# Sliding-window branch: two heads per evacuation, query copies on GpSimd, and the late weight loads on another queue

## The chip, the cores and the metric

One core of one Trainium2 chip runs the whole program. The metric is the device time of one execution in microseconds; a lower time is better. The kernel before takes 2685.36 us (median of three runs, 2685.33 to 2692.31).

## The reference

Two attention branches read the same 2048 x 640 input and a gate mixes them:

```python
g = sigmoid((x * gate_w).sum(-1))
a = A(x)        # 32 heads of width 20, query i sees keys i-255..i, output projection 640 x 640
b = B(x, mem0)  # 64 segments of 32 tokens, one after the other, 32 heads of width 192
out = g * a + (1 - g) * b
```

In branch B each segment is joined with 8 memory tokens, goes through the projections Wq, Wk, Wv, attention and Wo, and its first 8 output rows are the memory of the next segment. So the 64 segments form a chain. All tensors are bfloat16.

## The kernel before, in words

The program has four stages, one after the other on TensorE.

**The sliding branch** (`branch_A`) walks over 16 query blocks of 128 rows. A block sees up to `nk` = 3 key blocks of 128 keys (1 in the first block, 2 in the second). For each of the 32 heads there are three steps. `st_scores` makes the 128 x 384 scores in one PSUM bank (three products and two more that add the masks), VectorE takes the row maximum (`a_nmx`), and ScalarE writes the exponentials (`a_ex`). `st_transpose` turns the three 128 x 128 pieces on TensorE into a PSUM tile `pt_ps`, and one instruction copies that tile to SBUF (`a_pt`): ScalarE for two heads of three, VectorE for the third. `st_pv` multiplies with the values into `o_ps`. The loop over `i` issues scores of head `i`, the transpose of head `i-3` and the value product of head `i-5`. The scores have five PSUM buffers, `pt_ps` has two (pool `ps_t`), `o_ps` has one.

A query block needs its projections first. `prep_units` gives them as seven pieces, and the pieces for block `qb+1` are put between the heads of block `qb`. The query piece (`mk_qk` with `isq`) writes `QT_blk` on ScalarE and then four copies `QTm` per 16 heads (20 partitions x 512 elements each, the other partitions stay zero), eight copies in a block. `QTm` exists twice, so those of block `qb+1` are written while block `qb` computes. At the end of a block the result is transposed (`aT_ps`), copied (`aT`), multiplied with `wo` (`out_ps`), scaled by the gate (`ga`) and stored.

GpSimd has little to do in a block: it clears and fills `xs`, writes the column of ones of `V_blk`, and in the first blocks it issues DMAs: the first 30 weight tiles of branch B that stay in SBUF (`early`), and the copies of the streamed tiles into a packed DRAM tensor (`w_packed`).

**The tail products** (`tail_projections`) project the last 8 rows of every segment ahead of time, because they do not depend on the memory. First come the q and k products: four groups `g`, four column tiles `t`, six PSUM tiles of 20 products each (`t_psum`), copied alternately by ScalarE and VectorE to a staging tile `t_qk` (two buffers), which SyncE stores to DRAM as `xbqk`. Then come the v products (`t_psv`, `t_vt`, three buffers, stored as `xbv`). PSUM has eight tiles for both. One weight tile of each q and k group is streamed through `w_ring`.

Ahead of that stage the program loads the next weight tiles (`late`), and behind it the last two (`last`). Both are issued on SyncE's queue. A q, k or v tile is one DMA, an o tile is four.

**The memory branch** (`branch_B`) is a chain of 64 segments in an order written out by a planner of its own; it streams 21 weight tiles per segment from `w_packed` on SyncE's queue. **The mix** (`mix_out`) ends the program.

Outside of branch B the framework sets the order of the instructions on each engine: it lists them by the order in which they are written and by when its own plan has them ready, so the order in a queue differs from the text of the program. Each queue is then executed strictly in that order, and an instruction that waits holds up all behind it.

The lines that the change touches are 130 to 132 (query copies), 198 to 208 (transposes and their copies), 229 to 235 (the loop), 859 (the split of the weight tiles) and 880 to 887 (their loads).

Of the kernel before, what the change touches and what calls it, by code (L numbers as in the profile page):

```python
# [9 lines left out]
BF = mybir.dt.bfloat16  # L10
# [7 lines left out]
def branch_A(tc, x, wqkv, wo, gate_w, spread_x, ga_dram, omg_dram, W=256, HA=32, extra_units=None):  # L18
    nc = tc.nc
    S, D = x.shape  # L20
    P = 128
    KT = D // P
    DH = D // HA
    NB = S // P
    NG = HA // 4
    NKB = W // P + 1
# [3 lines left out]
    with ExitStack() as ctx:  # L30
# [50 lines left out]
        qms = {}  # L81

        def prep_units(qb):
# [31 lines left out]
            def mk_qk(isq, g0):  # L115
                def u():
                    xT = stt['xT']
                    Wp = WqP if isq else WkP
                    ng = min(4, NG - g0)
                    pst = ps_s.tile([P, 512], FP32, name="qk_ps", tag="s")  # L120
                    for gg in range(ng):
                        g = g0 + gg
                        for kt in range(KT):
                            nc.tensor.matmul(pst[:, gg * P:(gg + 1) * P],  # L124
                                             lhsT=Wp[:, kt, 4 * g:4 * g + 4, :].rearrange("p h d -> p (h d)"),
                                             rhs=xT[:, kt, :], start=(kt == 0), stop=(kt == KT - 1))
                    src = pst[:, 0:ng * P].rearrange("p (g q) -> p g q", q=P)
                    if isq:
                        nc.scalar.mul(stt['QT'][:, g0:g0 + ng, :], src, scale)
                        for r in range(4):  # L130
                            nc.vector.tensor_copy(qms[qb][r][32 * r:32 * r + DH, g0:g0 + ng, :],
                                                  stt['QT'][32 * r:32 * r + DH, g0:g0 + ng, :])
                    else:
                        nc.vector.tensor_copy(stt['KTb'][:, g0:g0 + ng, :], src)  # L134
                        if g0 + ng >= NG:
                            kring[qb] = stt['KTb']
                return u
# [27 lines left out]
        for qb in range(NB):  # L165
# [30 lines left out]
                hs[h] = dict(ex=ex)  # L196

            def st_transpose(h):
                ex = hs[h]['ex']
                pt_ps = ps_t.tile([P, NKB, P], BF, name="pt_ps", tag="t")  # L200
                for ci in range(nk):
                    nc.tensor.transpose(pt_ps[:, ci, :], ex[:, ci * P:(ci + 1) * P], ident[:])  # L202
                pt = hp.tile([P, NKB, P], BF, name="a_pt")
                if h % 3 != 2:
                    nc.scalar.copy(pt[:, 0:nk, :], pt_ps[:, 0:nk, :])  # L205
                else:
                    nc.vector.tensor_copy(pt[:, 0:nk, :], pt_ps[:, 0:nk, :])
                hs[h]['pt'] = pt

            def st_pv(h):  # L210
                pt = hs[h]['pt']
# [14 lines left out]
            nu = len(nxt)  # L226
            every = max(1, (HA - 4) // max(1, nu))
            ui = 0
            for i in range(HA + 5):
                if i < HA:  # L230
                    st_scores(i)
                if 0 <= i - 3 < HA:
                    st_transpose(i - 3)
                if 0 <= i - 5 < HA:
                    st_pv(i - 5)
                if ui < nu and i >= 2 and (i - 2) % every == 0:
                    nxt[ui](); ui += 1
# [20 lines left out]
P = 128  # L258
# [566 lines left out]
def kernel(  # L825
# [30 lines left out]
    xo_dram = dram.tile([nseg, P, KT * SEG], BF, name="xo_dram")  # L856
    streamed = [(k, g, c) for k in KINDS for g in range(4) for c in STREAMED[k][g]]
    weights = Weights(nc, dram, B_Wq, B_Wk, B_Wv, B_Wo, streamed)
    early, late, last = weights.resident[:30], weights.resident[30:-2], weights.resident[-2:]
    pre = ctx.enter_context(tc.tile_pool(name="b_pre", bufs=1))  # L860
    units = [lambda u=u: weights.load_resident(pre, u, nc.gpsimd) for u in early]
    units += [lambda u=u: weights.pack(u, nc.gpsimd) for u in streamed]
    with tc.tile_pool(name="b_xtail", bufs=1) as xtail:
        xTb = xtail.tile([P, KT, nseg * MEM], BF, name="xTb")
        with tc.tile_pool(name="b_xs", bufs=2) as xsp:

            def spread_x(qb, xT):
                n = P // SEG
                xv = xT[:].rearrange("p k (s a t) -> p s a k t", s=n, t=MEM)
                xs = xsp.tile([P, n, KT, SEG], BF, name="xs")  # L870
                nc.gpsimd.memset(xs[:], 0.0)
                for i in range(n):
                    nc.gpsimd.tensor_copy(xs[:, i, :, MEM:SEG], xT[:, :, i * SEG:(i + 1) * SEG - MEM])
                nc.sync.dma_start(xa_dram[qb * n:(qb + 1) * n].rearrange("s p c -> p s c"),
                                  xs[:].rearrange("p s k t -> p s (k t)"))
                nc.gpsimd.tensor_copy(xTb[:, :, qb * n * MEM:(qb + 1) * n * MEM].rearrange("p k (s t) -> p s k t", t=MEM), xv[:, :, 3])

            branch_A(tc, x, A_wqkv, A_wo, gate_w, spread_x, ga_dram[:], omg_dram[:], extra_units=units)
        post = ctx.enter_context(tc.tile_pool(name="b_post", bufs=1, side="right"))
        for u in late:  # L880
            weights.load_resident(post, u, nc.sync)
        tail_projections(tc, weights, xTb, xbqk, xbv)

    with ExitStack() as inner:
        end = inner.enter_context(tc.tile_pool(name="b_end", bufs=1))
        for u in last:
            weights.load_resident(end, u, nc.sync)
        branch_B(inner, tc, xa_dram, xbqk, xbv, mem0, weights, xo_dram)
    mix_out(tc, xo_dram, omg_dram[:], ga_dram[:], outf)

# [34 lines left out]
```

## Time and profile before

| | |
|---|---|
| median of three runs | 2685.36 us |
| the profiled execution | 2690.68 us, span 2689.0 us |
| sliding branch | 0 to 559.6 us |
| tail products | 559.6 to 771 us |
| memory branch and mix | 771 to 2689 us |
| busy share of the span | TensorE 85%, VectorE 45%, ScalarE 43%, GpSimd 18% |
| mean granted TensorE clock | 0.921 |

The stages are read from the timeline: the first tail product starts at 559.6 us, and the first streamed weight load of the memory branch is issued at about 771 us. The busy shares are averages over stages with different limits. From one full-size block of the sliding branch to the next everything in the trace returns after 34.1 to 34.4 us; the last such step takes 38.6 us.

### The profile page before, as it was taken

To read this page: it belongs to the slowest core of one execution; us is meant where nothing else is said; L and a number is where in the kernel's file an instruction comes from. 1 tells how busy PE (TensorE), PEld (TensorE's weight loads), DVE (VectorE), ACT (ScalarE), POOL (GpSimd) and SP (SyncE) were. 2 spreads that over 40 slices of the span, in tenths; PEclk is the share of its full clock that TensorE was granted. 3 is DMA by queue.
4 is the path that set the end of the run, shared out by engine and by line. 5 is a ranking of instruction groups with operands and counts; after the bars stand their busy time and mean duration, and the time that the engine had idled before them with its cause. 6 is when DMAs were issued, how large, how long until landed. Compare 5 with 4: busy or idle time off the path is not lost.

```text
span 2689.0 us, 114071 instructions
## 1 busy us (share of the span) xinstructions
PE 2289.0 (85%) x49893; PEld 1690.2 (63%) x49893; DVE 1212.2 (45%) x3738; ACT 1156.9 (43%) x2657; POOL 484.0 (18%) x1579
## 2 busy tenths in 40 slices
PE   6888888858978888888888888898888888888885
PEld 5777777657745665566566665666565656566663
DVE  6777777622233443443443443343344334334433
ACT  4777777722223333333333333343333333334333
POOL 6300000000011212222222222222222222122210
PEclk9888888888988988999999999899999999899987
DMA  7300000055568888888888888888888888888887
GB/s 275 103 17 17 17 17 14 10 169 159 146 207 258 269 268 264 287 283 279 279 273 292 281 272 273 276 283 285 275 272 274 271 272 276 259 277 280 281 263 232
DMA packets 303060, 591.78 MB, mean 220 GB/s; under 512 B 102552, under 2 KB 115616, under 8 KB 302560
## 3 DMA queue, kind: packets, MB, share of 16 engines
q1 hardware_dynamic: 282752, 537.49, 63.4%
q0 software_dynamic: 16848, 43.54, 5.0%
q8 instruction: 391, 6.41, 1.0%
q10 hardware_dynamic: 2960, 3.44, 0.4%
q14 instruction: 109, 0.89, 0.1%
HBM read 554.98 MB, written 36.97 MB: 220 GB/s over the span
## 4 chain that ended last, share of the span: by engine, by line
PE 51%; DMA 32%; ACT 9%; DVE 4%; issue 3%; SPq 1%; POOL 0%; ACTq 0%; DVEq 0%; POOLq 0%
DMA t_w<-w_packed 29%; PE ps_q L592 8%; PE ps_k L592 8%; PE ps_o L757 8%; PE ps_v L592 5%; ACT a_ex L195 4%; PE t_psum L433 3%; ACT a_pt L205 2%; PE ps_pv L733 2%; PE tr_k L607 2%; PE qk_ps L124 2%; PE pt_ps L202 2%; PE out_ps L250 2%; PE S_ps L661 2%; PE t_psv L450 1%
## 5 line engine op out<-in xcount | busy, mean ns | idle before, releaser
L592 PEld LDWEIGHTS <-t_hT 128*32 128x32 bf16 x15360 | 382.0, 99 | 316.2 <-issue 108.7
L757 PE MATMUL ps_o<-t_OT,t_w 128*128 128x40 bf16 x6400 | 270.5, 182 | 120.3 <-DMA t_w<-w_packed 110.4
L757 PE MATMUL ps_o<-t_OT,w_o 128*128 128x40 bf16 x8960 | 335.1, 182 | 41.7 <-ACT t_OT L738 41.7
L195 ACT ACTIVATE a_ex<-s_ps,a_nmx 128x384 bf16<-128x384 f32 (+2 forms) x512 | 288.9, 613 | 76.4 <-DVE a_nmx L193 76.0
L757 PEld LDWEIGHTS <-w_o 128*128 128x128 bf16 x8960 | 289.9, 98 | 49.1 <-issue 43.2
L757 PEld LDWEIGHTS <-t_w 128*128 128x128 bf16 x6400 | 210.7, 98 | 149.3 <-DMA t_w<-w_packed 146.2
L738 ACT CAST t_OT<-ps_pv 128x480 bf16<-128x480 f32 x256 | 142.9, 558 | 336.0 <-PE ps_pv L733 335.9
L193 DVE TENSOR_REDUCE a_nmx<-s_ps 128x1 f32<-128x384 f32 (+2 forms) x512 | 253.9, 525 | 29.8 <-PE s_ps L190 21.4
L597 ACT CAST t_tok<-ps_k 128x384 bf16<-128x384 f32 x256 | 122.5, 478 | 317.6 <-PE ps_k L592 317.6
L716 DVE TENSOR_TENSOR t_PTx<-PT_ps,mk_x 128x320 bf16<-128x320 f32 x256 | 125.2, 489 | 270.4 <-PE PT_ps L709 270.4
L592 PE MATMUL ps_q<-w_q,t_hT 128*32 128x384 bf16 x4096 | 229.7, 348 | 18.7 <-DVE t_hT L768 18.4
L592 PE MATMUL ps_v<-w_v,t_hT 128*32 128x384 bf16 x4352 | 231.7, 337 | 0.0
L639 POOL COPY t_K<-t_xqk 128x64 bf16<-128x64 bf16 x256 | 60.4, 236 | 950.5 <-PE S_ps L661 671.3
L592 PE MATMUL ps_k<-w_k,t_hT 128*32 128x384 bf16 x4096 | 228.0, 345 | 0.0
L187 PE MATMUL s_ps<-KT_blk,QTm 128*128 128x128 bf16 x1440 | 193.0, 227 | 2.5 <-DVE KT_blk L134 1.7
L202 PE MATMUL pt_ps<-a_ident,a_ex 128*128 128x128 bf16 x1440 | 161.4, 220 | 39.2 <-ACT a_pt L205 24.7
L630 DVE COPY t_K<-tr_k 128x256 bf16<-128x256 bf16 x256 | 74.0, 289 | 262.2 <-PE tr_k L607 260.9
L597 ACT CAST t_tok<-ps_q 128x384 bf16<-128x384 f32 x256 | 122.9, 480 | 145.0 <-PE ps_q L592 144.6
L205 ACT COPY a_pt<-pt_ps 128x384 bf16<-128x384 bf16 (+2 forms) x352 | 175.3, 508 | 18.2 <-PE pt_ps L202 13.9
L597 ACT CAST t_vtok<-ps_v 128x384 bf16<-128x384 f32 x256 | 122.4, 478 | 118.1 <-PE ps_v L592 117.4
L607 PEld LDWEIGHTS <-t_tok 128*128 128x128 bf16 x1536 | 88.1, 98 | 118.7 <-issue 55.4
L768 DVE CAST t_hT<-ps_o 128x40 bf16<-128x40 f32 x63 | 12.6, 200 | 320.9 <-PE ps_o L757 320.9
(136 smaller groups left out, 4601.3 us busy)
## 6 DMA issues: line engine op xcount, KB each, us to landing
t_w<-w_packed SPq DMA_DIRECT2D x704, 384.0 KB, 4.2
t_w<-w_packed SPq DMA_DIRECT2D x640, 320.0 KB, 4.2
xbqk<-t_qk SPq DMA_DIRECT2D x16, 768.0 KB, 4.3
t_xqk<-xbqk POOLq DMA_DIRECT2D x64, 192.0 KB, 4.7
w_v<-in_B_Wv_dram SPq DMA_DIRECT2D x17, 384.0 KB, 9.1
w_q<-in_B_Wq_dram POOLq DMA_DIRECT2D x16, 384.0 KB, 7.1
xbv<-t_vt SPq DMA_DIRECT2D x64, 96.0 KB, 1.8
t_xv<-xbv POOLq DMA_DIRECT2D x128, 48.0 KB, 4.5
```

The source lines that it names most:

```text
L187: nc.tensor.matmul(sp[:, ci * P:(ci + 1) * P], lhsT=qm[r][:, g, :], rhs=kring[c][:, g, :], start=True, stop=not need_mask)
L193: nc.vector.tensor_reduce(out=nmx[:], in_=sp[:, 0:nk * P], axis=AX.X, op=ALU.max, negate=True)
L195: nc.scalar.activation(out=ex[:, 0:nk * P], in_=sp[:, 0:nk * P], func=ACT.Exp, bias=nmx[:], scale=1.0)
L202: nc.tensor.transpose(pt_ps[:, ci, :], ex[:, ci * P:(ci + 1) * P], ident[:])
L205: nc.scalar.copy(pt[:, 0:nk, :], pt_ps[:, 0:nk, :])
L433: nc.tensor.matmul(pt[:, bb, :], lhsT=ws[ki][kt][:, c:c + P], rhs=xTb[:, kt, t * P:(t + 1) * P], start=(kt == 0), stop=(kt == KT - 1))
L592: nc.tensor.matmul(t[32 * j:32 * j + 32, 0:384], lhsT=tile_of(hT)[:, kt, :], rhs=w[:, j * 384:(j + 1) * 384], start=(kt == kts[0]), stop=( ...
L597: sc.op("ACT", act(384), lambda: nc.scalar.copy(tile_of(tok)[:], b["tile"][:, 0:384]), reads=[b], writes=[tok])
L607: nc.tensor.transpose(t[:, k, :], tok["tile"][:, k * P:(k + 1) * P], ident[:])
L716: nc.vector.tensor_tensor(out=tile_of(dst)[:], in0=PT["tile"][:, i, :, :].unsqueeze(2).to_broadcast([P, 2, 4, L]), in1=mk.unsqueeze(1).uns ...
L738: sc.op("ACT", act(480), lambda: nc.scalar.copy(tile_of(OT)[:].rearrange("p b j l -> p (b j l)"), o["tile"][:, 0:480]), reads=[o], writes= ...
L757: nc.tensor.matmul(t[:, dt * L:(dt + 1) * L], lhsT=w[:, r * D + dt * P:r * D + (dt + 1) * P], rhs=OT["tile"][:, b, i, :], start=(g == 0 an ...
```

## The change

Three things change.

1. Transposes and their copies go by pairs of heads. `st_transpose` does nothing for an even head; for an odd head it transposes both heads of the pair into one PSUM tile of twice the size and copies it with one instruction, ScalarE for every other pair and VectorE for the rest. The copied tile has four buffers of two heads in place of eight of one. `st_pv` runs for two heads in every second turn of the loop.
2. The eight query copies `QTm` of a block are issued on GpSimd in place of VectorE.
3. Four more weight tiles are loaded early (34 in place of 30), and the remaining `late` and `last` loads are issued on GpSimd's queue in place of SyncE's.

```diff
@@ mk_qk
                         for r in range(4):
-                            nc.vector.tensor_copy(qms[qb][r][32 * r:32 * r + DH, g0:g0 + ng, :],
+                            nc.gpsimd.tensor_copy(qms[qb][r][32 * r:32 * r + DH, g0:g0 + ng, :],
                                                   stt['QT'][32 * r:32 * r + DH, g0:g0 + ng, :])
@@ st_transpose
             def st_transpose(h):
-                ex = hs[h]['ex']
-                pt_ps = ps_t.tile([P, NKB, P], BF, name="pt_ps", tag="t")
-                for ci in range(nk):
-                    nc.tensor.transpose(pt_ps[:, ci, :], ex[:, ci * P:(ci + 1) * P], ident[:])
-                pt = hp.tile([P, NKB, P], BF, name="a_pt")
-                if h % 3 != 2:
-                    nc.scalar.copy(pt[:, 0:nk, :], pt_ps[:, 0:nk, :])
+                if h % 2 == 0:
+                    return
+                pt_ps = ps_t.tile([P, 2, NKB, P], BF, name="pt_ps", tag="t")
+                for a in range(2):
+                    ex = hs[h - 1 + a]['ex']
+                    for ci in range(nk):
+                        nc.tensor.transpose(pt_ps[:, a, ci, :], ex[:, ci * P:(ci + 1) * P], ident[:])
+                pt = hp.tile([P, 2, NKB, P], BF, name="a_pt", bufs=4)
+                if h % 4 == 1:
+                    nc.scalar.copy(pt[:, :, 0:nk, :], pt_ps[:, :, 0:nk, :])
                 else:
-                    nc.vector.tensor_copy(pt[:, 0:nk, :], pt_ps[:, 0:nk, :])
-                hs[h]['pt'] = pt
+                    nc.vector.tensor_copy(pt[:, :, 0:nk, :], pt_ps[:, :, 0:nk, :])
+                for a in range(2):
+                    hs[h - 1 + a]['pt'] = pt[:, a]
@@ the loop over heads
-            for i in range(HA + 5):
+            for i in range(HA + 6):
                 if i < HA:
                     st_scores(i)
                 if 0 <= i - 3 < HA:
                     st_transpose(i - 3)
-                if 0 <= i - 5 < HA:
+                if 0 <= i - 5 < HA and i % 2 == 0:
+                    st_pv(i - 6)
                     st_pv(i - 5)
@@ the kernel
-    early, late, last = weights.resident[:30], weights.resident[30:-2], weights.resident[-2:]
+    early, late, last = weights.resident[:34], weights.resident[34:-2], weights.resident[-2:]
@@
         for u in late:
-            weights.load_resident(post, u, nc.sync)
+            weights.load_resident(post, u, nc.gpsimd)
         tail_projections(tc, weights, xTb, xbqk, xbv)
@@
         for u in last:
-            weights.load_resident(end, u, nc.sync)
+            weights.load_resident(end, u, nc.gpsimd)
```

## The prediction

> **What bounds the kernel now.** I read the page first, then windows by stage, then the chain of waits inside one block of the sliding branch, the grouped lines by form, and the queues of SyncE and GpSimd around the tail products.
>
> ```profile
> PE 2289.0 (85%) x49893; PEld 1690.2 (63%) x49893; DVE 1212.2 (45%) x3738; ACT 1156.9 (43%) x2657; POOL 484.0 (18%) x1579
> ...
> 0.00:559.60 559.60, 474.82 (x7120) 398.82 (x7121) 397.88 (x1018) 413.31 (x961) 88.27 (x213) 0.90 0.18 58
> 559.60:771.00 211.40, 164.85 (x2261) 141.30 (x2261) 50.95 (x81) 43.19 (x80) 6.54 (x25) 0.89 0.58 166
> 771.00:2689.00 1918.00, 1649.35 (x40520) 1150.09 (x40511) 763.35 (x2639) 700.40 (x1616) 389.15 (x1341) 0.93 0.86 273
> ```
>
> Columns of a window: length, busy of PE, PE loads, DVE, ACT, POOL, clock, DMA share, GB/s. The change touches the first two rows, 771 us; the third (1918 us) has the same instructions before and after, and I put it at zero. In the first row ACT and DVE are busy 74% and 71%, far above their 43% and 45% of the page.
>
> One block of the sliding branch, from the chain of waits and the waits of two blocks:
>
> ```profile
> by line: ACT a_ex L195 19.3%; ACT a_pt L205 11.5%; PE qk_ps L124 11.1%; PE pt_ps L202 8.7%; PE out_ps L250 8.1%; PE s_ps L187 7.2%; DVE a_nmx L193 6.1%; issue 6.0%; PE s_ps L190 4.9%; DVE a_pt L207 2.8%; DVE QTm L131 2.5%; PE o_ps L217 2.3%
> ...
> 445.45 0.37 ACT a_pt L205
> ...
> 448.48 0.36 DVE a_pt L207
> ...
> 448.89 0.34 PE pt_ps L202 x3
> ...
> 449.31 0.49 ACT a_pt L205
> ...
> 455.49 0.11 PE s_ps L187
> ...
> ACT a_ex L195 <- DVE a_nmx L193: 9.7, 6, 4.1
> PE pt_ps L202 <- ACT a_pt L205: 3.3, 8, 0.7
> ```
>
> A block has 27 us in which heads run (scores from 421.4, one 34.1 us period before 455.49, to the last exponential at 448.48) and 7 us of ending (448.48 to 455.49: last copy, value product, `aT`, `out_ps`). In the 27 us ScalarE waits little: of its 9.7 us in two blocks for the row maximum, 4.1 per block is the block's first. It is the bound there, with VectorE close behind.
>
> ```profile
> L205 ACT COPY a_pt<-pt_ps 128x384 bf16<-128x384 bf16 x286 | 146.3, 521 | 15.4 <-PE pt_ps L202 11.8 <-remote 2.9 <-PE s_ps L190 0.2
> ...
> L207 DVE COPY a_pt<-pt_ps 128x384 bf16<-128x384 bf16 x130 | 45.7, 351 | 18.7 <-ACT a_ex L195 18.3
> ...
> L205 ACT COPY a_pt<-pt_ps 128x256 bf16<-128x256 bf16 x22 | 8.3, 394 | 1.3 <-PE pt_ps L202 1.2
> ...
> L207 DVE COPY a_pt<-pt_ps 128x256 bf16<-128x256 bf16 x10 | 2.9, 285 | 1.5 <-PE pt_ps L202 1.3
> ...
> 432.07 1.18 DVE L131 COPY QTm<-QT_blk 20x512 bf16<-20x512 bf16 x4
> ...
> 433.95 0.22 PE L187 MATMUL s_ps<-KT_blk,QTm 128*128 128x128 bf16 x1
> ...
> 434.48 0.22 PE L187 MATMUL s_ps<-KT_blk,QTm 128*128 128x128 bf16 x1
> ```
>
> The tail products, on SyncE's queue, TensorE, GpSimd's queue and the chain:
>
> ```profile
> 562.51 14.73 SPq L382 DMA_DIRECT2D w_v<-in_B_Wv_dram  x17
> 577.88 34.49 SPq L387 DMA_DIRECT2D w_o<-in_B_Wo_dram  x48
> 612.49 6.90 SPq L442 DMA_DIRECT2D xbqk<-t_qk  x3
> ...
> 617.69 0.58 PE L433 MATMUL t_psum<-xTb,w_q 128*128 128x128 bf16 x4 [35.47 <-ACT t_qk L438]
> ...
> 617.69 6.09 PE t_psum L433 x80
> ...
> 624.88 6.24 DMA w_ring<-w_packed
> ...
> 631.17 73.81 PE t_psum L433 x1316
> ...
> 761.82 1.12 SPq L387 DMA_DIRECT2D w_o<-in_B_Wo_dram  x2
> ...
> 770.54 4.32 SPq L560 DMA_DIRECT2D t_w<-w_packed  x5
> ...
> 771.05 5.18 DMA t_w<-w_packed
> ...
> 779.59 0.27 PE S_ps L654
> ...
> 769.84 0.57 POOL L546 DMA_DIRECT2D t_xqk<-xbqk  x1 [3.71 <-DMA xbv<-t_vt]
> ```
>
> The first three stores of `xbqk` stand behind 65 load issues and leave at 612.49, though the tiles were ready long before. Both `t_qk` buffers are full, the eight PSUM tiles fill, and TensorE stops for 35.47 us, from 582.2 to 617.7.
>
> **The change part by part.**
>
> *Copies by pairs.* ScalarE issues 21.3 copies a block at 0.37 us from start to start, 7.9 us. From 256 to 384 elements a copy grows by 127 ns, so 384 more cost 0.38 us: eight copies of 0.75 us, 6.0 us. ScalarE gains 1.9 us a block. VectorE goes from 10.7 copies of 0.26 (0.36 in the chain less the 0.1 us by which the next begins early), 2.8 us, to eight of 0.46 (66 ns per 128 elements, 0.20 us more each), 3.7 us: it loses 0.9 us. TensorE issues the same products. Each `pt_ps` buffer now holds two heads, so the wait of `pt_ps` for ScalarE's copy (3.3 us in two blocks) should shrink. In the ending, the last transposes no longer wait for VectorE's copy of the head two before (0.36 us), but there are six and their copy is longer (351 + 198 = 549 ns on VectorE against 490): I count nothing.
>
> *Query copies.* VectorE loses eight at 0.29 us, 2.35 us a block; with the 0.9 above it gains 1.4. On GpSimd:
>
> ```profile
> L876 POOL COPY xTb<-xT_blk 128x160 bf16<-128x160 bf16 x16 | 5.2, 325 | 0.0
> ...
> L66 POOL COPY WkP<-wqk_stage 128x640 bf16<-128x640 bf16 x5 | 4.1, 828 | 4.5 <-DMA wqk_stage<-in_A_wqkv_dram 4.5
> ...
> POOL V_blk L147 <- PE o_ps L217: 58.1, 2, 29.1
> ...
> L387 POOL DMA_DIRECT2D w_packed<-in_B_Wo_dram x40 | 20.3, 515 | 0.1
> ```
>
> Between these rows 512 elements come to 0.69 us, so 5.5 us a block; GpSimd now waits 29 us a block for nothing but the value column, and the copies are ready some 20 us before the next block reads them. Hidden. Without that cover (behind the `V_blk` memset, which waits for the block's last value products, about 450.5, and the `xs` copies of some 2.5 us) they would run from 453 to 458.5; the next block begins at 455.49 and needs only the first four for its first 16 heads: under 1 us a block. In the first block they are on the path; GpSimd starts issuing weights there too. 8 x (0.69 - 0.29) = 3.2 us lost at most, against the key copies that VectorE now makes at once: 0.
>
> *Block sum.* ScalarE's 1.9 us is the most a block can gain while ScalarE bounds it; the least is nothing. TensorE's own work is 32 x 0.53 us for heads (from one head's first score product, 433.95, to the next's, 434.48), an estimated 6 us of projections for the next block (80 products at 0.056 us and the values) and 1 us more for the low clock of the start (0.11 us a product at 455.49): 24 of the 27 us, and VectorE has 1.4 us more room. So neither stops the gain, but both are near. I take two thirds, 1.3 us, and 15 full blocks' worth (the short first ones count less): -20 us, ends 0 and -29.
>
> *Late loads.* On SyncE the stall of 35.5 us goes. The 80 products after it took 6.09 us at a low clock, against 80 x 0.0561 = 4.5 at the rate of the 1316: another 1.6. What is late next is the stores beside the loads. GpSimd issues 15 v tiles and 48 pieces; in the early part it paced the big ones by their landing:
>
> ```profile
> 32.48 0.54 POOL L382 DMA_DIRECT2D w_q<-in_B_Wq_dram  x1 [0.42 <-DMA w_q<-in_B_Wq_dram]
> 33.46 0.54 POOL L382 DMA_DIRECT2D w_q<-in_B_Wq_dram  x1 [0.44 <-DMA w_q<-in_B_Wq_dram]
> ...
> xbqk<-t_qk SPq DMA_DIRECT2D x16, 768.0 KB, 4.3
> ...
> w_ring<-w_packed SPq DMA_DIRECT2D x11, 384.0 KB, 3.4
> ...
> 638.00:645.00 7.00, 7.00 (x129) 7.00 (x127) 2.07 (x3) 2.06 (x4) 0.00 (x0) 1.00 0.45 120
> ```
>
> About 1 us for each v tile (32.48 to 33.46), so from 562 to 577, then 48 x 0.55 us, to 604. The first store can leave at 567, after 120 products at 0.056 us from 559.6 and a copy. It needs 3.2 us of all DMA engines (0.45 of 7 us); if the nine v tiles still to come all go ahead of or beside it, it lands near 579, before 582.2, where TensorE stopped. So no stall. The streamed tile for the second group lands beside the loads: 6.2 us, as in the chain above, in place of the usual 3.4: +3. At the end the eight `w_o` issues (4.3 us) no longer stand between the last `xbv` stores and the first `t_w`; on GpSimd they move `t_xqk` by at most 0.4 beyond its 3.7 us wait, and the first scores (779.59) start 3.4 us after the first `t_w` lands (776.2). -4. The four tiles loaded early cost 4 x 0.54 us on an idle queue: 0. Tail: -35.5 - 1.6 - 4 + 3 = -38.
>
> A rule of the Trainium skill speaks against this move: "DMA: Bandwidth & Descriptors", section "SWDGE vs HWDGE vs iDMA", says that DMAs from GpSimd and from SyncE sit in different queues inside each DMA engine, which takes turns between them. By it a store of small pieces advances one piece per large weight piece, and its landing would be near my 12 us rather than the 4.3 us shown; the sum stays -38, since 579 is before 582.2. No run so far shows the two together.
>
> **Sum.** The profiled execution took 2690.7 us, 5.3 above the median. -20 - 38 = -58 gives 2632.7 for such an execution and 2627 for the median.
>
> **The rivals.**
> - *The sliding branch gains nothing.* Bunched transposes and value products make TensorE wait for the longer copy, or TensorE takes over as the bound; its 24 of 27 us speak for it. -38 alone: 2647. Chance 0.20.
> - *The loads starve the stores.* The first `xbqk` store lands only when the `w_o` pieces too are through, at about 606, and TensorE stands still from 582 as now. 24 us of the stall come back: -20 - 14, 2651. Against it: the pieces come at 0.55 us per 80 KB, 145 GB/s, half of what the memory branch moves (273 GB/s in the windows above). Chance 0.10.
> - *More comes through in the sliding branch.* All of ScalarE's 1.9 us and the 1 us in which it now waits inside a block, 2.7 x 15 = 40: 2607. Chance 0.10.
> - *Slower than before.* The pair's copy is queued on ScalarE behind exponentials, the value products of two heads wait for it in TensorE's strict order, and the next scores behind them come late, so each pair pays the wait. A copy now has 0.75 us in place of 0.37; if 0.3 us of each of the 16 pairs lands on the path, a block loses 4.8 us and 15 lose 72: 2685 + 72 - 38 = 2719. It decides from 38 / 15 = 2.5 us a block, 0.16 us a pair. Against it: the five score buffers let TensorE run ahead. Chance 0.10, near its turning point as often as beyond.
>
> **How the numbers follow.** My forecast (both parts pay) has 0.50. The range 2606 to 2655 takes in the forecast, the first two rivals and half of the third, 0.8 after some rest for errors of size. A measurement tells 0.3%, 8 us, from no change. Faster 0.90: all cases but the last, which is split into same 0.04 and slower 0.06.
>
> **What would show it.** Right: the block period falls from 34.1 to about 32.8 us; `a_pt` has 256 copies, ScalarE's near 0.87 us each; `QTm` copies on GpSimd of about 0.7 us, with no wait of `s_ps` for them; no TensorE gap over 5 us between 560 and 705 on the old scale, `xbqk` leaving every 6.7 us; the first `t_w` 4 us sooner after the last v product. Wrong: a wait of `o_ps` for `a_pt` in each pair, a gap of `t_psum` waiting for `xbqk`, or a longer memory branch, which I put at no change without having worked it out.

## The result, and the profile after

The changed kernel takes 2618.04 us (median of three runs, 2616.62 to 2625.68) against 2685.36 us before: 67.3 us less, ratio 0.9749 with a 95% interval of 0.9711 to 0.9786. The forecast was 2627, the range 2606 to 2655. The profiled execution took 2625.68 us with a span of 2624.0 (before: 2690.68 and 2689.0), so 65.0 us are to be found in the traces.

The page of the changed kernel, and its windows by stage: length, then busy time of TensorE, its weight loads, VectorE, ScalarE and GpSimd, then clock, DMA share and GB/s.

```profile
PE 2259.0 (86%) x49877; PEld 1665.6 (63%) x49893; DVE 1189.0 (45%) x3578; ACT 1115.8 (43%) x2433; POOL 602.1 (23%) x1782
...
xbqk<-t_qk SPq DMA_DIRECT2D x16, 768.0 KB, 5.1
```
```profile
0.00:523.15 523.15, 447.41 (x7105) 374.88 (x7122) 374.76 (x858) 371.70 (x737) 167.42 (x345) 0.95 0.21 65
523.15:708.80 185.65, 166.49 (x2245) 143.28 (x2244) 50.95 (x81) 43.29 (x80) 42.86 (x95) 0.95 0.65 187
708.80:2624.00 1915.20, 1645.06 (x40528) 1147.45 (x40528) 763.30 (x2639) 700.79 (x1616) 391.78 (x1342) 0.94 0.86 273
```

Set against the three rows of before: the sliding branch ends at 523.2 in place of 559.6 us, and the clock in it is 0.95 in place of 0.90. The third row has the same instructions as before and is 2.8 us shorter; where its left edge is put moves it by as much.

To compare many kernels the stages are cut at instructions: the first tail product, the first v product, and the first output product (`ps_o`) of the memory branch. "q and k" goes from the first of these to the second, "tail" from the first to the third, "rest" from there to the end (us, profiled executions).

| kernel | sliding | q and k | tail | rest |
|---|---|---|---|---|
| before | 559.6 | 145.2 | 227.4 | 1902.0 |
| changed | 523.1 | 117.8 | 197.8 | 1903.1 |
| difference | -36.5 | -27.4 | -29.6 | +1.1 |
| e1 loads only | 558.3 | 118.5 | 196.4 | 1885.6 |
| e2 sliding only | 528.8 | 144.6 | 226.8 | 1879.9 |
| e3 pairs only | 528.1 | 146.8 | 230.8 | 1884.3 |
| e4 queries only | 553.3 | 145.5 | 226.3 | 1909.1 |
| e5 pair buffers | 552.6 | 116.7 | 196.8 | 1882.2 |
| e6 o pieces first | 523.4 | 118.5 | 199.3 | 1898.8 |
| e7 paced, SyncE | 526.8 | 133.1 | 213.4 | 1882.0 |
| e8 warm | 517.5 | 117.4 | 197.4 | 1885.8 |
| e9 changed again | 526.4 | 116.2 | 194.7 | 1887.2 |
| e10 paced, GpSimd | 523.7 | 121.5 | 201.3 | 1873.6 |
| e11 paced and warm | 512.4 | 122.2 | 201.8 | 1874.4 |
| e12 before, warm | 544.9 | 144.8 | 225.4 | 1902.6 |

The rest moves between 1874 and 1909 us though every kernel does the same work there. Whole times carry that spread, so the stages are what tells the parts apart.

**Inside a block.** The groups of two blocks of the changed kernel:

```profile
L195 ACT ACTIVATE a_ex<-s_ps,a_nmx 128x384 bf16<-128x384 f32 x64 | 32.8, 597 | 7.7 <-DVE a_nmx L193 7.7
...
L208 ACT COPY a_pt<-pt_ps 128x768 bf16<-128x768 bf16 x16 | 13.0, 812 | 3.7 <-PE pt_ps L205 3.6
L221 PE MATMUL o_ps<-V_blk,a_pt 128*128 128x21 bf16 x192 | 9.8, 174 | 2.2 <-ACT a_pt L208 1.6
...
L131 POOL COPY QTm<-QT_blk 20x512 bf16<-20x512 bf16 x16 | 9.7, 609 | 14.9 <-ACT QT_blk L129 14.2
L210 DVE COPY a_pt<-pt_ps 128x768 bf16<-128x768 bf16 x16 | 8.8, 553 | 3.3 <-PE pt_ps L205 3.0
```

ScalarE now makes 8 copies a block, 812 ns each. Transposes no longer appear with a wait for `a_pt`: in the kernel before they waited 3.3 us in two blocks. The value products wait a little more: in the same two blocks 2.2 us against 0.7 before, and their weight loads 5.3 against 1.4, mostly for ScalarE's copy (six products and twelve weight loads of 32 pairs, 0.5 us at the longest). The query copies take 609 ns on GpSimd, and no score product waits for them.

Windows one block long, one of before and two of the changed kernel, these from one gate multiplication (`ga`) to the next:

```profile
353.00:387.10 34.10, 30.21 (x470) 25.65 (x469) 25.24 (x64) 26.77 (x60) 2.08 (x8) 0.90 0.06 17
```
```profile
265.71:296.83 31.12, 27.32 (x470) 23.45 (x469) 23.95 (x53) 24.01 (x46) 6.97 (x15) 1.00 0.06 18
361.89:394.77 32.88, 29.54 (x469) 25.21 (x469) 24.38 (x53) 24.21 (x46) 6.94 (x15) 0.92 0.06 18
```

ScalarE is busy 24.0 us a block in place of 26.8, VectorE 24.0 in place of 25.2. But the two blocks of the same kernel differ by 1.8 us, and the column that goes with it is the clock. The twelve full blocks before the long one, by period and clock:

| kernel | periods, us (clock) |
|---|---|
| before | 34.1 to 34.4 (0.90), all twelve |
| changed | 31.1 to 31.4 (0.98 to 1.00) in six, 32.4 to 32.9 (0.92) in six |
| e4 queries only | 34.1 to 34.2 (0.85) in six, then 33.4 to 33.9 (0.90 to 0.91) in six |
| e5 pair buffers | 33.7 (0.96), 33.7 to 33.9 (0.90 to 0.91) in five, then 34.1 (0.90) in six |
| e8 warm | 31.5 (1.00), all twelve |
| e11 paced and warm | 31.2 (1.00), all twelve |
| e12 before, warm | 32.7 to 32.9 (0.97 to 1.00) in five, 33.3 to 34.0 (0.95 to 0.98) in seven |

The clock is lost in the ending. The chain of waits in two endings of the changed kernel, first with the clock full and then with it halved (start, length, what):

```profile
455.20 0.70 ACT aT L250
455.90 0.27 issue
456.18 1.04 PE out_ps L255 x4
...
459.60 0.06 PE s_ps L190
```
```profile
391.67 0.70 ACT aT L250
392.37 0.45 issue
392.82 2.45 PE out_ps L255 x9
395.27 0.11 PE s_ps L187
395.37 0.11 PE s_ps L190
```

In the second the next block's scores wait for nine output products (2.45 us) and begin at 0.11 us a product, twice the 0.06 that a score product takes in the first.

**The tail.** The chain of waits of the changed kernel, then TensorE's two stops in it, then what GpSimd issued:

```profile
523.15 7.99 PE t_psum L438 x120
...
531.77 17.23 DMA xbqk<-t_qk
...
549.87 2.31 PE t_psum L438 x20
552.17 0.02 issue
552.19 6.87 DMA w_ring<-w_packed
559.05 0.05 issue
559.10 6.94 PE t_psum L438 x92
```
```profile
549.87 0.59 PE L438 MATMUL t_psum<-xTb,w_q 128*128 128x128 bf16 x4 [3.11 <-DVE t_qk L445]
...
559.10 0.23 PE L438 MATMUL t_psum<-xTb,w_ring 128*128 128x128 bf16 x1 [2.76 <-DMA w_ring<-w_packed]
```
```profile
525.85 5.32 POOL L387 DMA_DIRECT2D w_v<-in_B_Wv_dram  x10 [56.39 <-DMA ga_dram<-ga]
531.53 0.54 POOL L387 DMA_DIRECT2D w_v<-in_B_Wv_dram  x1 [0.37 <-DMA w_v<-in_B_Wv_dram]
```

The stop of 35.47 us is gone; 3.11 and 2.76 us have taken its place. The first store left at 531.77 as soon as its tile was ready, but took 17.23 us to land, because ten v tiles had been issued in one burst just before. The DMA view from 532 to 550 us (packets, MB, share of 16 engines) shows both queues at work at once, GpSimd's (q0) and SyncE's (q1):

```profile
q0 software_dynamic: 1170, 5.08, 72.7%
q1 hardware_dynamic: 3998, 1.52, 33.3%
```

### The profile page after: what moved, and what is told of

Read it like the earlier page. It is cut to its first block, busy times and chain, and to the rows that moved or that the text cites. A ratio compares the mean times of both kernels' runs of the same rounds, so it can differ in the third digit from the quotient of the medians.

```text
span 2624.0 us, 113795 instructions
## 1 busy us (share of the span) xinstructions
PE 2259.0 (86%) x49877; PEld 1665.6 (63%) x49893; DVE 1189.0 (45%) x3578; ACT 1115.8 (43%) x2433; POOL 602.1 (23%) x1782
## 4 chain that ended last, share of the span: by engine, by line
PE 51%; DMA 35%; ACT 10%; DVE 2%; issue 2%; SPq 0%; ACTq 0%; POOL 0%; DVEq 0%
DMA t_w<-w_packed 32%; PE ps_q L597 8%; PE ps_k L597 8%; PE ps_o L762 7%; PE ps_v L597 5%; ACT a_ex L195 4%; PE t_psum L438 4%; ACT a_pt L208 3%; PE qk_ps L124 3%; PE ps_pv L738 2%; PE tr_k L612 2%; PE t_psv L455 2%; PE S_ps L666 2%; PE pt_ps L205 1%; PE s_ps L187 1%
## 5 line engine op out<-in xcount | busy, mean ns | idle before, releaser
L195 ACT ACTIVATE a_ex<-s_ps,a_nmx 128x384 bf16<-128x384 f32 (+2 forms) x512 | 252.8, 576 | 64.2 <-DVE a_nmx L193 61.5
L193 DVE TENSOR_REDUCE a_nmx<-s_ps 128x1 f32<-128x384 f32 (+2 forms) x512 | 246.7, 523 | 32.4 <-PE s_ps L190 24.8
L597 PE MATMUL ps_k<-w_k,t_hT 128*32 128x384 bf16 x4096 | 226.3, 343 | 0.3
L187 PE MATMUL s_ps<-KT_blk,QTm 128*128 128x128 bf16 x1440 | 171.0, 223 | 6.0 <-ACT a_ex L195 5.6
L205 PE MATMUL pt_ps<-a_ident,a_ex 128*128 128x128 bf16 x1440 | 145.6, 220 | 8.5 <-ACT a_ex L195 1.2
L676 DVE TENSOR_REDUCE sm_mx<-S_ps 128x4 f32<-128x160 f32 x256 | 82.5, 322 | 149.0 <-PE S_ps L666 149.0
```

The costliest lines, as they stand in the source:

```text
L187: nc.tensor.matmul(sp[:, ci * P:(ci + 1) * P], lhsT=qm[r][:, g, :], rhs=kring[c][:, g, :], start=True, stop=not need_mask)
L193: nc.vector.tensor_reduce(out=nmx[:], in_=sp[:, 0:nk * P], axis=AX.X, op=ALU.max, negate=True)
L195: nc.scalar.activation(out=ex[:, 0:nk * P], in_=sp[:, 0:nk * P], func=ACT.Exp, bias=nmx[:], scale=1.0)
L205: nc.tensor.transpose(pt_ps[:, a, ci, :], ex[:, ci * P:(ci + 1) * P], ident[:])
L597: nc.tensor.matmul(t[32 * j:32 * j + 32, 0:384], lhsT=tile_of(hT)[:, kt, :], rhs=w[:, j * 384:(j + 1) * 384], start=(kt == kts[0]), stop=( ...
L676: nc.vector.tensor_reduce(out=x["mx"][:], in_=view(), axis=AX.X, op=ALU.max)
```

## The experiments

The theory after the result: the two halves of the change add up; in the sliding branch the single long copy per pair pays and the moved query copies do not; what came beyond the forecast there is clock; and the tail fell short because the burst of loads slows the first store. Rivals: the gain comes from the pair buffers (TensorE no longer waiting for a copy), or from VectorE's relief, or from the even split of the copies (16 heads on ScalarE in place of 22) and not from their length; and the tail's rest is lost to something other than the burst. e1 to e4 ran on one chip with one set of runs of the kernel before (median 2679.14, 2664.72 to 2694.74), e5 to e8 on another with one execution each (before 2691.55), e9 to e12 on a third (before 2686.88, 2678.99 to 2700.78).

**e1, the loads alone**, on the kernel before:

```diff
-    early, late, last = weights.resident[:30], weights.resident[30:-2], weights.resident[-2:]
+    early, late, last = weights.resident[:34], weights.resident[34:-2], weights.resident[-2:]
...
-            weights.load_resident(post, u, nc.sync)
+            weights.load_resident(post, u, nc.gpsimd)
... (the same for `last`)
```

> The kernel before with the third part alone: 34 tiles early, the late and last loads on GpSimd's queue. Theory (two independent gains): the sliding branch keeps its 34.1 us per block and ends at 559.6 us; the stage of tail products, from its first product to the first product of the memory branch, falls from 216.7 to the 185.7 us of the changed kernel; the whole is some 31 us faster, 2654 us. Rival (the gains lean on each other: with the early loads or the free SyncE queue the sliding branch itself got faster): the first tail product comes clearly before 555 us, and the whole is more than 40 us faster.

Measured: 2648.73 us, ratio 0.9899 (0.9836 to 0.9961). The tail is 31.0 us shorter (196.4 against 227.4), the sliding branch 1.3. Its chain shows the same store:

```profile
558.33 7.07 PE t_psum L433 x120
...
566.04 17.71 DMA xbqk<-t_qk
```

The slow store comes with the loads, not with the sliding branch.

**e2, the sliding branch alone**: the changed kernel with 30 early tiles and the late and last loads on `nc.sync`.

> The kernel before with pairs of heads and the query copies on GpSimd, loads as before. Theory (two independent gains): the sliding branch ends near 523 us as in the changed kernel, the stall of 35 us in the tail products stays, the whole is 36 us faster, 2649 us. Rival (part of the sliding gain comes from the loads): it ends later than 530 us.

Measured: 2641.14 us, ratio 0.9859 (0.9808 to 0.9909). Sliding branch -30.8, tail -0.6: it ends at 528.8, between the 523 of the theory and the 530 of the rival, and near what the same branch shows in five other runs (523.1 to 526.8). The halves do not touch each other's stage: 0.9899 times 0.9859 is 0.976, the whole change gave 0.9749.

**e3, pairs without the query copies.** It was built on e2, with the loads as in the kernel before; its tail is therefore that of the kernel before, and it is to be compared with e2.

```diff
-                            nc.gpsimd.tensor_copy(qms[qb][r][32 * r:32 * r + DH, g0:g0 + ng, :],
+                            nc.vector.tensor_copy(qms[qb][r][32 * r:32 * r + DH, g0:g0 + ng, :],
```

> The changed kernel with the query copies back on VectorE. Theory (ScalarE and the two transpose buffers bound a block, VectorE does not): blocks stay at 31.1 to 32.8 us, the first tail product comes within 5 us of 523. Rival (VectorE is as near to the bound as ScalarE): the 2.35 us of query copies come back on the path, blocks of 33 to 35 us, the first tail product at 540 us or later.

Measured: 2646.27 us, 0.988 (0.9828 to 0.9932). The sliding branch ends at 528.1 against e2's 528.8, with blocks of the same 31.1 to 32.9 us. Windows of e2 and of e3 over the branch:

```profile
0.00:528.80 528.80, 452.44 (x7104) 380.27 (x7121) 375.81 (x858) 371.94 (x737) 165.52 (x341) 0.93 0.20 61
```
```profile
0.00:528.10 528.10, 452.17 (x7104) 378.04 (x7121) 411.50 (x986) 373.19 (x737) 88.47 (x213) 0.93 0.19 61
```

VectorE does 35.7 us more in e3 (third busy time) and the branch is no longer. VectorE's load is not what the block waits for, and moving the query copies adds nothing measurable to a full block on top of the pairs. At the start of the program it does: the first block's `ga` begins at 50.3 us in e3 and at 47.8 in e2. In all four kernels with the copies on VectorE it begins at 49.2 to 51.0, in all ten with them on GpSimd at 46.8 to 48.5. In the whole branch this gain is covered by e2's longer block late in the branch (37.9 us against 34.7).

**e4, the query copies alone**, the same line moved to GpSimd in the kernel before.

> The kernel before with the query copies on GpSimd and nothing else. Theory (ScalarE and the transpose buffers bound a block): under 0.4 us a block, the first tail product at 554 us or later, the whole within 0.3% of before. Rival (VectorE is as near to the bound): 1 us a block or more, the first tail product before 545 us.

Measured: 2679.06 us, 0.9986 (0.9954 to 1.0017): no change. The sliding branch is 6.3 us shorter in the profile; the table above shows blocks 0.2 to 0.7 us shorter at about the old clock of 0.90, and six that fell to 0.85 and gained next to nothing. Of the 6.3 us, 1.8 lie ahead of the first `ga` (48.25 against 50.07) and 1.1 in the interval behind it.

**e5, the pair's buffers without the long copy**, in the changed kernel; the copies are made by single heads again, two of three on ScalarE:

```diff
-                if h % 4 == 1:
-                    nc.scalar.copy(pt[:, :, 0:nk, :], pt_ps[:, :, 0:nk, :])
-                else:
-                    nc.vector.tensor_copy(pt[:, :, 0:nk, :], pt_ps[:, :, 0:nk, :])
+                for a in range(2):
+                    if (h - 1 + a) % 3 != 2:
+                        nc.scalar.copy(pt[:, a, 0:nk, :], pt_ps[:, a, 0:nk, :])
+                    else:
+                        nc.vector.tensor_copy(pt[:, a, 0:nk, :], pt_ps[:, a, 0:nk, :])
```

> The changed kernel, both heads of a pair still transposed into one double-size PSUM tile, but copied by one instruction for each head, on ScalarE for two heads of three as before. Theory (ScalarE's own work bounds a block): ScalarE has its 1.9 us a block back, blocks return to 33 to 34.5 us, the first tail product comes at 540 us or later. Rival (the waits for a free transpose buffer were the cost, and the pair tile ends them): blocks stay at 31.1 to 32.9 us, the first tail product within 5 us of 523.

Measured: 2633.32 us, sliding branch 552.6, blocks of 33.7 to 34.1 us. Groups of two of its blocks:

```profile
L209 ACT COPY a_pt<-pt_ps 128x384 bf16<-128x384 bf16 x44 | 21.8, 534 | 3.5 <-PE pt_ps L205 3.2
L205 PE MATMUL pt_ps<-a_ident,a_ex 128*128 128x128 bf16 x192 | 18.5, 220 | 0.6
```

The transposes wait 0.6 us in all, against 3.3 for ScalarE's copies alone in the kernel before, and the block is as long as before or 0.4 us shorter. So the wait of `pt_ps` was harmless, and the rival of the buffers falls. What pays is that ScalarE has less to copy: 8 long copies a block in place of 22 short ones.

e5 does not tell why that is less, because it undoes two things at once, the length of the copies and the even split: 22 of 32 heads are ScalarE's again, where the changed kernel gives it 16. Rows of before and of the changed kernel have the price of one copy, from its start to the start of the next instruction:

```profile
372.03 0.49 ACT L205 COPY a_pt<-pt_ps 128x384 bf16<-128x384 bf16 x1
372.39 0.61 ACT L195 ACTIVATE a_ex<-s_ps,a_nmx 128x384 bf16<-128x384 f32 x1
```
```profile
276.07 0.79 ACT L208 COPY a_pt<-pt_ps 128x768 bf16<-128x768 bf16 x1
276.75 1.54 ACT L195 ACTIVATE a_ex<-s_ps,a_nmx 128x384 bf16<-128x384 f32 x3
```

A short copy costs 0.36 us, a long one 0.68 here and 0.70 at the median, nearly as much as two short ones. By these rows ScalarE's copies fall from 22 x 0.36 = 7.9 us a block to 8 x 0.70 = 5.6, and 16 short ones would cost 5.8: about nine tenths of ScalarE's relief are an estimate for the even split, one tenth for the joining. No run splits the copies evenly without joining them, so what joining alone brings is not shown. (The branch as a whole is 7.0 us shorter than before, about what e4, which shares the query copies with it but neither pairs nor late loads, has too.)

**e6, the `w_o` pieces ahead of the v tiles** in the late loads of the changed kernel:

```diff
-        for u in late:
+        for u in sorted(late, key=lambda u: u[0] != "o"):
```

> The changed kernel with the late loads in another order on GpSimd's queue: the 48 small pieces of the o tiles first, the 15 v tiles behind them. Theory (the first store is slowed to 17.2 us by v tiles that fill the DMA engines; the pieces, bound by their issue, do not fill them): the first xbqk store lands in 5 to 8 us, the stall of 3.1 us near 547 us goes, and the slow landings move to where the v tiles now come, some 28 us later. Rival (any load beside a store slows it as much): the first store again takes over 12 us.

Measured: 2623.19 us; q and k 118.5, as in the changed kernel. The DMA view from 523 to 535 us has the first store beside the small pieces, and the chain has it later beside the v tiles:

```profile
xbqk<-t_qk SPq DMA_DIRECT2D x1, 768.0 KB, 6.3
```
```profile
562.87 18.13 DMA xbqk<-t_qk
```

Beside `w_o` pieces the store takes 6.3 us; beside v tiles 18.1. That ties the slowness to the burst of v tiles. Turning the order round only moves the stop to where they come.

**e7, the loads paced by the stores**, on SyncE: two late tiles behind each `xbqk` store.

```diff
... (`sto` is the store of `xbqk`; the loop over `late` ahead of the stage is gone)
+                with tc.issue_after(sto.ins):
+                    for u in late[:2]:
+                        weights.load_resident(post, u, nc.sync)
+                del late[:2]
```

> The changed kernel with the late loads on SyncE's queue again, but two tiles behind each xbqk store in place of all at once; the last two tiles stay on GpSimd. Theory (loads in a burst slow the stores, and each stall brings low clock): no store over 8 us, no stall of t_psum, q and k products in 108 to 111 us in place of 117.8. Rival (the low clock and the stalls have other causes): 115 us or more. If the issues on SyncE hold up the stores: some t_psum wait for a store beyond 1 us.

Measured: 2623.89 us, q and k 133.1: a miss. No store takes over 8.6 us, but now the streamed tile stands behind the loads on SyncE's queue:

```profile
592.02 0.29 PE L438 MATMUL t_psum<-xTb,w_ring 128*128 128x128 bf16 x1 [8.60 <-DMA w_ring<-w_packed]
```
```profile
623.32 6.30 SPq L392 DMA_DIRECT2D w_o<-in_B_Wo_dram  x8
629.74 0.99 SPq L413 DMA_DIRECT2D w_ring<-w_packed  x2
```

The eight issues of 6.30 us end just before `w_ring` leaves at 629.74, and TensorE's next product starts at 633.12 after 12.34 us of waiting. It is the old mistake on a smaller scale: a load issue in front of a transfer that is due.

**e8, the ending kept busy**, in the changed kernel: 48 products of a constant tile, which nobody reads, spread over the last six turns of the head loop.

```diff
+            def keep_warm(n):
+                w = ps_s.tile([P, 512], FP32, name="warm", tag="s")
+                for _ in range(n):
+                    nc.tensor.matmul(w[:, 0:P], lhsT=ident[:], rhs=m_last[:], start=True, stop=True)
...
+                if i >= HA:
+                    keep_warm(8)
```

> The changed kernel with 48 products without use on TensorE in the ending of each block (masks times identity into a score buffer that nothing reads), between the last transposes, value products and the transposes of the result. Theory (blocks of 32.6 to 32.9 us are those whose ending falls into windows of low clock, because TensorE idles there): every full block near 31.1 to 31.5 us at clock 1.0, the sliding branch 8 to 12 us shorter than 523 us. Rival (the low clock is not set by the idle ending, or the added products hold up the path as much as they bring): 520 us or more.

Measured: 2602.4 us, sliding branch 517.5. Every block before the long one has the full clock and the same period:

```profile
380.00:411.50 31.50, 29.50 (x518) 26.09 (x516) 23.82 (x53) 23.98 (x48) 6.95 (x15) 1.00 0.06 18
```

So the two sorts of block of the changed kernel are one sort with and without the clock. The branch is 5.6 us shorter than the changed kernel's 523.1, where 8 to 12 were expected: the blocks take 31.5 us, 0.3 to 0.4 more than those of the changed kernel at the full clock (31.1 to 31.2).

**e9, the changed kernel once more**, unaltered, beside the last three.

> The changed kernel once more, unaltered, for a comparison on one chip with the two that follow. Expected: sliding branch to 523 to 529 us, q and k products near 118 us with one store landing in about 17 us, ratio to before near 0.975.

Measured: 2613.97 us, 0.9726 (0.9694 to 0.9758), sliding branch 526.4, q and k 116.2, the slowest store 17.4 us. With e6, e7, e10 and e2, which have the same sliding branch, its end lies between 523.1 and 528.8: which blocks get the full clock, and the length of the long block (34.1 to 37.9 us in these), differ by run.

**e10, the loads paced on GpSimd**, each pair of tiles behind a one-element copy from the staging tile:

```diff
... (behind the store of `xbqk`; the loop over `late` ahead of the stage is gone)
+                tick = vst.tile([P, 1], BF, name="t_tick")
+                tk = nc.gpsimd.tensor_copy(tick[:], st[:, HS - 1, 1, 11, MEM - 1:MEM])
+                with tc.issue_after(tk.ins):
+                    for u in late[:2]:
+                        weights.load_resident(post, u, nc.gpsimd)
```

> The changed kernel with the late loads still on GpSimd's queue, but two tiles behind each group of t_qk: a one-element copy out of the finished t_qk tile on GpSimd lets the next two load issues go. SyncE's queue stays free. Theory (a burst of loads slows the first stores, and the stalls bring low clock): no store over 9 us, no stall for a store, q and k products in 109 to 113 us in place of 117.8, which is 5 to 9 us of the whole. Rival (the second group's streamed tile and the clock at the start make up the difference, not the burst): 115 us or more.

Measured: 2625.49 us, 0.9751 (0.9713 to 0.9789); q and k 121.5 against 116.2 in e9. A second miss, on its rival's side (115 us or more). No store takes over 7.6 us and none stops TensorE; the waits from 523 to 645 us show what does (total, times, longest):

```profile
PE t_psum L438 <- DMA w_ring<-w_packed: 8.2, 3, 3.5
```

Spread-out loads are beside all three later streamed tiles, the burst was beside one. The same bytes must come in while the q and k products run, and each way of ordering them has its own transfer that is late. With the burst the total is smallest.

**e11, e10 with the ending kept busy** by 38 products (8, 8, 6, 4, 4, 8).

> The paced loads of the kernel above and the products without use in the ending of each block, 38 in place of 48 and fewer of them right ahead of the transposes. Theory: blocks of 31.1 to 31.4 us, all at full clock, and q and k products in 109 to 113 us; 12 to 18 us faster than the changed kernel, ratio to before near 0.969. Rival (fewer products let the low clock return): blocks of 32.6 us again in some places.

Measured: 2598.42 us, 0.9678 (0.9643 to 0.9713), the lowest median of its chip, 15.6 us below e9's; the intervals of the two overlap a little. Its sliding branch is 14.0 us shorter than e9's:

```profile
394.00:425.20 31.20, 28.86 (x508) 25.57 (x507) 23.99 (x54) 24.02 (x47) 6.32 (x14) 1.00 0.04 13
```

The paced loads give it nothing (q and k 122.2, a miss). The useless products with the loads in a burst should be the better of the two; 38 products with the burst were not run.

**e12, the kernel before with the ending kept busy** by 34 products.

> The kernel before with 34 products without use in the ending of each block. Theory (a window of low clock costs a block of the sliding branch some 1.5 us wherever it falls into ending and start): its blocks fall from 34.1 to 32.3 to 32.8 us without any part of the change. Rival (ScalarE alone sets the block before, so the clock does not matter there): 33.8 us or more.

Measured: 2674.59 us in one run. The sliding branch ends at 544.9, 14.7 us earlier, with no other change to it. The theory's 32.3 to 32.8 us is met by one block only: five take 32.7 to 32.9 us and seven 33.3 to 34.0, three of these at or beyond the rival's 33.8, because 34 products do not hold the full clock everywhere (0.95 to 0.98 in the seven). Its two blocks at 1.00:

```profile
244.81:277.75 32.94, 29.58 (x504) 25.91 (x503) 25.09 (x63) 26.79 (x60) 2.11 (x7) 1.00 0.06 18
377.88:410.55 32.67, 29.47 (x504) 25.93 (x503) 25.09 (x63) 26.79 (x60) 2.10 (x7) 1.00 0.06 18
```

They take 32.9 and 32.7 us. At the full clock the pairs and query copies are then worth 32.8 - 31.2 = 1.6 us a block (31.2 is e11's block).

## Why the prediction was right, and where its sizes were off

The side was right. That the time came so near was luck in part: two errors of opposite sign cancelled. Forecast for the profiled execution: -20 and -38. Measured: -36.5 and -29.6, and +1.1 in the rest.

*Copies by pairs: right, with the right bound.* ScalarE was named as the bound. e5 and e3 show it: the buffers alone and VectorE's relief alone bring next to nothing, and ScalarE's smaller copy work brings the gain. The count that the price was set on was off: ScalarE made 22 copies a block and VectorE 10, not 21.3 and 10.7, because the count of heads starts anew in every block (the rows of the 256-element block have x22 and x10). And the gain was put down to the longer copy, which the prediction's own prices do not bear out: 16 short copies at 0.37 us are 5.9 us, as much as eight long ones at 0.75, so the even split alone would give the same. That was not run (see e5). The forecast block of 32.8 us is what the blocks at clock 0.92 take (32.4 to 32.9), and at about equal clock the gain is 1.2 to 1.8 us (34.1 to 32.4 and 32.9; e12's 32.7 and 32.9 to 31.1) where 1.3 was taken. The reckoned price of a copy, 0.75 us from start to start, was near: the chain has `a_pt` at 0.70 to 0.84 us, and 812 ns for the whole instruction where 0.87 was expected. TensorE did not stop the gain, and the value products' wait for ScalarE's copy is 1.6 us in two blocks, in six of 32 pairs, not 0.3 us in each: the slower rival and the rival of no gain both fall.

*The missed term: the clock in the ending.* I took the half-rate stretch of each ending as given. Split over the twelve full blocks: six at 0.92 gained about 1.6 us each, six at 0.98 to 1.00 gained 3.0, together 27.3 us. About 1.6 us a block, 19 us, is the copies; the other 8 us is clock that half of the blocks no longer lose. The other 9.2 us of the 36.5 are the start (2.9), the first interval (1.7), the long block (3.9) and the last (0.7). e8, e11 and e12 show the clock's part by itself: with the ending kept busy all twelve blocks of e8 and of e11 have one length, and the kernel before gains 14.7 us from that alone. The rival "more comes through" came near the size of the branch's gain (-40) by a wrong cause, more of ScalarE's time.

Why half of the blocks is an inference. The half-rate stretches in the blocks of these two traces last 3.41 us or twice that (in e4 also three times), and the block of before, 34.1 us, is ten times 3.41: its twelve stretches start 34.1 us apart, so each ending met the raster in the same place, and lost the same. At 31.1 us the place moves from block to block, and only some endings are hit. The Trainium skill, "TensorE: Matmul & The Clock Gate", Part 1, has a free-running window of 3.4 us and half rate after an idle window. The trace agrees on the length, with stretches of 3.41 us, but not on the idleness: in the 3.41 us ahead of a half-rate stretch TensorE is still busy for half of the time.

```profile
344.30:347.71 3.41, 1.84 (x35) 1.61 (x34) 0.80 (x2) 2.95 (x8) 0.00 (x0) 1.00 0.00 0
347.71:354.54 6.83, 5.71 (x40) 3.62 (x37) 2.88 (x7) 0.97 (x3) 2.10 (x7) 0.50 0.20 51
354.54:357.95 3.41, 3.41 (x60) 2.96 (x58) 3.23 (x11) 3.41 (x9) 0.00 (x0) 1.00 0.13 48
```

These are windows of the kernel before: 35 products at the full clock, 40 in twice that time at half, then 60 again. That e5's blocks go from 33.7 to 34.1 us and stay there fits the inference; that e4's stood at 34.1 to 34.2 us for six blocks and then left for 33.4 to 33.9 shows that the place does not hold for good. No run moved the raster on purpose.

*Query copies: hidden, as forecast, and without value in a full block.* 609 ns each against 0.69. The 1.4 us of VectorE were no part of what the block waited for once pairs are used. The first block was put at nothing, 3.2 us of slower copies against the key copies that VectorE makes at once. There they pay: VectorE's first key copy (`KT_blk`) starts at 24.9 us in place of 26.6 and the first scores at 25.8 in place of 27.4, which is 1.6 of the 2.9 us at the start. All fourteen traces have it so: the first scores come at 25.8 to 26.8 us with the copies on GpSimd, at 27.4 to 28.1 with them on VectorE.

*Late loads: the stall went, two terms were mis-sized.* The first store was to land near 579 us, 12 us after it left, ahead of TensorE's stop. It took 17.23 us. The step that failed is the pacing of the v tiles: I had them one by one, about 1 us each and held by their landings, as in the early rows; GpSimd put out ten in 5.32 us before the store left. The early part of the kernel before had shown the same: eleven loads issued from 21.5 to 29.9 us before the first that waited for a landing, at 30.3; the rows that were read are the ones behind those. Cost: 3.11 us of stop, and low clock that I had not counted. The rows of the chain give it: 120 products in 7.99 us, 20 in 2.31 and 92 in 6.94, 17.2 us for what takes 13.0 at 0.0561 us each, 4.2 lost, 1.3 of them in the first 120, which run ahead of the stop. The w_ring term was right (2.76 against 3). Together q and k lose 3.1 + 2.8 + 4.2 = 10.1 us where I had 3, hence -27.4 instead of -34.1. The end gained 3.3 us where 4 was put (tail less q and k less v products: 25.2 before, 21.9 after); the v products took 1.1 more. The rival that the loads starve the stores had the right victim at an eighth of its price, 3.1 us of stop in place of 24, but named the wrong loads: it put the delay on the `w_o` pieces, beside which a store takes 6.3 us (e6), and not on the v tiles.

The rule that was weighed there, from the Trainium skill's "DMA: Bandwidth & Descriptors", section "SWDGE vs HWDGE vs iDMA", has each DMA engine take turns between the two queues. The trace agrees that the store is slowed, four times over. It does not show one piece of a store for each piece of a load, as the prediction reckoned: in the 18 us, 3998 packets of the stores' queue (two stores) went through for 1170 of the loads'.

*Memory branch: no change, as forecast,* within a spread of 35 us between profiled executions. The 0.3% that I took as what a measurement can tell was too little for one run: the kernel before alone ran from 2664.72 to 2694.74 us on one chip.

## What to carry to other kernels

Before a stage with many short instructions is changed, find the engine whose queue has no waits inside the period; less work there pays, whether by fewer instructions or by giving a part to an engine with room (price both from start to start before choosing), while buffers and relief on other engines may show waits going away and bring nothing. When a loop body ends in a short dependent chain, look at the clock column of the windows from one ending to the next: the ending may cost more in clock than in waiting, and some 40 useless products can be worth nearly as much as the change under study (14.7 us in e12 against some 19 us for the copies). When loads are moved off a queue, ask in what burst the new queue will send them, and which small transfer will share the DMA engines with that burst.

## What the runs showed of the hardware

- A block period near a multiple of the 3.41 us stretches can stay there: twelve blocks at 34.1 to 34.4 us in the kernel before, while with the full clock its block takes 32.7 to 32.9 (e12). In e4 six blocks stood at 34.1 to 34.2 us, and the next six did not.
- The half rate comes without a whole idle stretch: in the 3.41 us ahead of it TensorE was busy for 1.84 us with 35 products (kernel before, 344.30 to 347.71 us).
- A 768 KB store that lands in 4.3 us at the median of the kernel before takes 17.2 to 18.1 us beside 384 KB weight tiles and 6.3 us beside 80 KB pieces.
- GpSimd's queue took ten 384 KB loads, one each 0.53 us, before the first wait for a landing; in the early part of the kernel before it was eleven.
- One full block late in the branch is some 2 to 6 us longer than those ahead of it in every kernel (38.6 us before, 34.7 after, 34.1 to 38.8 in the others), with or without useless products (36.9 and 36.2 us in e8 and e11). In e2 there are 2.77 us in it in which no engine works; in the kernel before no such gap is longer than 0.1 us. Its cause stays open.
